# A start with x tiles 2 and 3 transposed by DMA, and K of both branches in pieces of 512, 512 and 256 columns, in a two-branch linear attention kernel

## The chip, the cores and the metric

The kernel runs on one core of a Trainium2 chip. The metric is the device time of one execution in microseconds (us). Each round of experiments ran on a chip of its own, beside its own runs of the kernel before. The profile also tells the granted clock, the share of full speed that TensorE was allowed. One execution of each kernel is also traced.

## The reference

Two attention branches A and B read the same x (2048 rows of 640, bf16) and differ in their weights. Each has 32 heads of 20 features. A gate per row mixes them.

```python
def branch(x, wqkv, wo):                      # A and B alike
    q, k, v = heads(x @ wqkv)
    phi = lambda t: jnp.where(t > 0, t + 1, jnp.exp(t)) + 1e-6
    pq, pk = phi(q), phi(k)
    kv  = jnp.einsum("bhsd,bhse->bhde", pk, v)
    z   = jnp.einsum("bhsd->bhd", pk)
    num = jnp.einsum("bhqd,bhde->bhqe", pq, kv)
    den = jnp.einsum("bhqd,bhd->bhq", pq, z)[..., None] + 1e-6
    return rows(num / den) @ wo
# x = A_x for both branches
g = sigmoid((x * gate_w).sum(-1, keepdims=True))
return g * branch(x, A_wqkv, A_wo) + (1 - g) * branch(x, B_wqkv, B_wo)
```

## The kernel before

x is cut into 16 tiles of 128 rows. The stages, in TensorE's order, are: K of every tile and branch (x^T times the K weights, then the feature map phi on ScalarE and VectorE); G = phi(K)^T x, summed over all tiles; M and WP, which fold the V weights and the output weights into G; the queries; the denominators (`dens`); the factors 1/den (`scale_q`); and the final products (`final`). A small list scheduler in the program orders the operations of each engine and picks PSUM banks. Each DMA has a semaphore of its own.

The start: single loads for tiles 0 to 3 of x, which TensorE transposes, and DMA transposes for the rest.

```python
        load_wk("SP", 4)
        load_x("ACT", 2)
        load_x("SP", 3)
        for c0, c1 in ((0, 1), (1, 3), (3, 5)):
            dma("SP", "wkB%d" % c0, WK["B"][:, c0:c1, :], weights("B", D, c0, c1), ...)
        for b in range(1, NB):            # x^T of tiles 4 to 15, four tiles each
            dma("SP", "xt%d" % b, XT[:, :, 512 * b : 512 * b + 512], ..., transpose=True)
        # ... constants, then the rows of x, four tiles each, then V, output and Q weights
```

K of a tile is made in two pieces of 320 columns for each branch (G of one k runs over all 16 tiles; its code is in the whole kernel below):

```python
        def k_part(X, t, tile, cs, chain=False):
            # ...
            def steps():
                return [
                    (PS[:, tile.banks[h], 0:HALF], XT[:, c, xc], WK[X][:, c, HALF * h : HALF * h + HALF], c == 0, c == NC - 1, None)
                    for h, c in order
                ]
```

The part that will matter although the change doesn't touch it: the factor 1/den is made by VectorE (`rc`), written to a DRAM scratch by SyncE (`fw`), read back spread over the partitions (`fr`), and multiplied into the query features by VectorE.

```python
            sch.op("DVE", rec, 1740, reads=[(ds,)], writes=[(ds,)], name="rc%d" % b)
            dma("SP", "fw%d" % b, rep..., lambda: RC[...], ...)            # factor <- RC
            dma("SP", "fr%d" % b, lambda: RX[...], rep..., ...)            # RX <- factor
            # for each piece and branch: VectorE, PQ = PQ * RX  ("ml")
# ... and the order of the second half of the kernel:
        d01 = dens(0)
        scale_q(0, d01, 2)
        queries(2)
        queries(3)
        scale_q(1, d01, 2)
        d23 = dens(2)
        finals(0)
```

In VectorE's program the multiplies of `scale_q(0)`, which wait for the read-back, stand in front of later feature maps of `queries(2)` and `queries(3)`, and those free TensorE's PSUM banks and feed `dens(2)`. The chain in experiment 1 shows them run in that order.

Of the kernel before, what the change touches and what calls it, by code (L numbers as in the profile page):

```python
# [19 lines left out]
D = 640  # L20
# [295 lines left out]
def bass_gated_mix__linear_attn_block__linear_attn_block__prompt_kernel(nc, A_x, A_wqkv, A_wo, B_x, B_wqkv, B_wo, gate_w, out):  # L316
# [6 lines left out]
    with ExitStack() as es:  # L323
        E = es.enter_context

        def sb(name, shape, dtype=dt.bfloat16):
            return E(nc.sbuf_tensor(name, shape, dtype))
# [4 lines left out]
        WK = {X: sb("WK" + X, [128, NC, D]) for X in XS}  # L332
        WV = {X: sb("WV" + X, [128, NC * D + 88]) for X in XS}
        WO = {X: sb("WO" + X, [128, 5, D]) for X in XS}
        FE = {X: sb("FE" + X, [128, NT * D]) for X in XS}
        PK = {X: FE[X][:, :].rearrange("p (t f) -> p t f", f=D) for X in XS}
        PQ = {X: FE[X][:, :].rearrange("p (k s) -> p k s", s=S) for X in XS}
# [102 lines left out]
        load_x("ACT", 2)  # L440
        load_x("SP", 3)
# [5 lines left out]
        for b in range(1, NB):  # L447
            dma(
                "SP", "xt%d" % b, XT[:, :, 512 * b : 512 * b + 512], xin[512 * b : 512 * b + 512, :],
                writes=[("XT", t) for t in range(4 * b, 4 * b + 4)], us=3.3, transpose=True,  # L450
            )
        dma("SP", "consts", CB[:, :], cap[:, :], writes=[("CB",)], us=0.3)
        dma("SP", "gw", GWB[:, :], gate_w.partition_broadcast(128), writes=[("GWB",)], us=0.4)
        for b in range(1, NB):
            dma(
                "SP", "xn_%d" % b, XN[:, 4 * b : 4 * b + 4, 0:D],
                xin[512 * b : 512 * b + 512, :].rearrange("(t p) f -> p t f", p=128),
                writes=[("XN", t) for t in range(4 * b, 4 * b + 4)], us=2.0,
            )
# [27 lines left out]
        def transpose_x(t):  # L487
# [11 lines left out]
            for c0, c1 in ((0, 2), (2, NC)) if t < 2 else ((0, NC),):  # L499
                sch.op(  # L500
                    "DVE",
                    lambda e, c0=c0, c1=c1: e.tensor_copy(  # L502
                        XT[:, c0:c1, 128 * t : 128 * t + 128],
                        PSB[:, tt.banks[0], 128 * c0 : 128 * c1].rearrange("p (c f) -> p c f", f=128),
                    ),
                    _dve_ns(128 * (c1 - c0)), reads=[(tt,)], writes=[("XTC", t, c) for c in range(c0, c1)], name="xev%d" % t,
                )
# [29 lines left out]
        def k_part(X, t, tile, cs, chain=False):  # L537
# [3 lines left out]
            def steps():  # L541
# [6 lines left out]
                "k%s%d_%d" % (X, t, cs[0]), steps, ([("XTC", t, c) for c in cs] if t < 4 else [("XT", t)]) + [("WK", X, c) for c in cs], [(tile,)], len(cs) * (D + 12),  # L548
                after=at[0] if chain else None,
            )  # L550
            if chain:
                at[0] = o

        gone = {}

        def g_unit(X, k):
            tile = _Tile(2)

            def steps():
                r = []  # L560
                for t in range(NT):
# [5 lines left out]
            gone[X] = mms(  # L567
                "g%s%d" % (X, k), steps,
                [("F", X, "k", t) for t in range(NT)] + [("XN", t) for t in range(NT)] + [("XN1",)], [(tile,)], NT * (D + 13),
            )  # L570
# [125 lines left out]
        def q_unit(X, b, k):  # L696
# [8 lines left out]
            over = [("F", X, "k", t) for t in range(span[0] // D, span[-1] // D + 1)]  # L705
# [7 lines left out]
            mms("q%s%d%d" % (X, b, k), steps, ([("XT", t) for t in range(4 * b, 4 * b + 4)] if b else [("XTC", t, c) for t in range(4) for c in range(NC)]) + [("WQ", X)], [(tile,)], NC * 518, after=gone[X])  # L713
# [151 lines left out]
        transpose_x(2)  # L865
# [3 lines left out]
        transpose_x(3)  # L869
        for t in (2, 3):  # L870
            first("A", *[(t, c) for c in range(NC)])
            phi_k("A", t, kt["A", t])
        for t in range(4):
            first("B", *[(t, c) for c in range(NC)])
            phi_k("B", t, kt["B", t])
        for b in range(1, NB):
            for X in XS:
                for t in range(4 * b, 4 * b + 4):
                    tile = _Tile(2)
                    k_part(X, t, tile, list(range(NC)), chain=True)  # L880
                    phi_k(X, t, tile)
# [85 lines left out]
```

## Time and profile before

| | before |
|---|---|
| time known at the prediction, three executions | 196.35, 194.47, 194.06 us, median 194.47 |
| execution that was traced | 193.3 us, span 191.5 us |
| TensorE busy | 187.0 us, 98% of the span |
| VectorE, ScalarE busy | 128.6 us (67%), 74.8 us (39%) |

Read the busy shares first: TensorE is at 98%, nothing else is near. Then read the chain that ended last. The prediction shows its beginning; here is its end (start us, duration us, what):

```profile
188.18 0.40 ACT TS L831
...
188.61 0.38 DVE OL L837
```

The last VectorE instruction ends at 188.61 + 0.38 = 188.99 us, and the span ends at 191.5. The 2.51 us between them are the last output's store and what comes after it. (The spans are printed to 0.1 us, so each such tail, as this stretch is called below, is good to 0.05 us.)

### The profile page before, as it was taken

The numbers are of one execution on the slowest core, as the hardware profiler recorded it, in microseconds if no ns is written. First come the engines' busy times: TensorE is split into PE (matmuls) and PEld (weight loads), VectorE is DVE, ScalarE is ACT, GpSimd is POOL, SyncE is SP. The second block draws the span as 40 slices with busy tenths as digits, with TensorE's granted clock in tenths as the row PEclk, the third lists the DMA queues.
The fourth block names the chain that finished last, engine by engine and source line by source line (L and its number), as shares of the span: only waits on it lengthen the run. The fifth ranks groups of instructions, "written<-read, shape, count | busy, mean of one in ns | idle before, by whom it ended". The sixth has DMA issues, their size and how long they took to land.

```text
span 191.5 us, 3302 instructions
## 1 busy us (share of the span) xinstructions
PE 187.0 (98%) x1370; PEld 131.8 (69%) x1370; DVE 128.6 (67%) x247; ACT 74.8 (39%) x115; POOL 8.2 (4%) x14
## 2 busy tenths in 40 slices
PE   7899999999999999999999999999999999999993
PEld 3677777777888888888855666455556677777773
DVE  1298888888700008996179997896999969923332
ACT  2154545555311111203255478565554331333232
POOL 8900000000000000000000000000000000000000
PEclk9999999999999999999999999999999999999999
DMA  5999999980011411121543004665000173221122
GB/s 173 330 211 185 180 388 364 311 216 17 3 34 34 38 34 34 34 38 34 38 90 107 0 24 172 162 223 170 0 0 0 38 218 104 78 96 64 39 72 68
DMA packets 30784, 21.17 MB, mean 111 GB/s; under 512 B 15538, under 2 KB 30514, under 8 KB 30770
## 3 DMA queue, kind: packets, MB, share of 16 engines
q1 hardware_dynamic: 30050, 20.23, 40.8%
q10 hardware_dynamic: 720, 0.74, 1.1%
q8 instruction: 11, 0.18, 0.4%
q14 instruction: 3, 0.02, 0.0%
HBM read 12.05 MB, written 5.31 MB: 91 GB/s over the span
## 4 chain that ended last, share of the span: by engine, by line
PE 95%; DMA 2%; ACTq 0%; DVE 0%; ACT 0%; issue 0%
PE ps L398 95%; DMA XN<-in_A_x_dram 2%; PE ps L493 1%; ACTq L387 0%; ACT TS L831 0%; DVE OL L837 0%; DVE XT L502 0%
## 5 line engine op out<-in xcount | busy, mean ns | idle before, releaser
L521 ACT ACTIVATE EK<-ps 128x640 bf16<-128x640 f32 x32 | 22.4, 703 | 24.1 <-PE ps L398 24.1
L715 ACT ACTIVATE EK<-ps 128x512 bf16<-128x512 f32 x40 | 23.9, 597 | 18.4 <-PE ps L398 17.0
L831 ACT ACTIVATE TS<-ps,GA 128x640 f32<-128x640 f32 (+2 forms) x18 | 13.2, 734 | 29.6 <-PE ps L398 29.6
L398 PE MATMUL ps<-WPB,FEB 128*128 128x320 bf16 (+1 forms) x165 | 24.7, 295 | 0.0
L398 PE MATMUL ps<-WPA,FEA 128*128 128x320 bf16 (+1 forms) x165 | 24.7, 295 | 0.0
L398 PE MATMUL ps<-WKA,XT 128*128 128x320 bf16 x160 | 22.9, 299 | 0.5 <-DMA WKA<-in_A_wqkv_dram 0.3
L398 PE MATMUL ps<-XT,WQA 128*128 128x512 bf16 x100 | 22.8, 380 | 0.0
L398 PE MATMUL ps<-XT,WQB 128*128 128x512 bf16 x100 | 22.7, 379 | 0.0
L398 PE MATMUL ps<-XN,FEB 128*128 128x320 bf16 (+1 forms) x160 | 22.5, 300 | 0.0
L398 PE MATMUL ps<-WKB,XT 128*128 128x320 bf16 x160 | 22.4, 299 | 0.0
L837 DVE SCALAR_TENSOR_TENSOR OS<-ps,GA,TS 128x640 bf16<-128x640 f32 x15 | 13.0, 867 | 13.4 <-PE ps L398 12.8
L398 PE MATMUL ps<-XN,FEA 128*128 128x320 bf16 (+1 forms) x160 | 22.0, 300 | 0.0
L572 ACT ACTIVATE GS<-ps 128x640 bf16<-128x640 f32 x10 | 7.0, 703 | 36.7 <-PE ps L398 36.7
L398 PEld LDWEIGHTS ps<-XN,FEA 128*128 128x128 bf16 x160 | 18.8, 117 | 3.0
L398 PEld LDWEIGHTS ps<-XN,FEB 128*128 128x128 bf16 x160 | 18.7, 118 | 3.0
L398 PEld LDWEIGHTS ps<-WKA,XT 128*128 128x128 bf16 x160 | 15.4, 98 | 7.0 <-DVE XT L502 1.3
L398 PEld LDWEIGHTS ps<-WPA,FEA 128*128 128x128 bf16 x165 | 15.9, 98 | 6.1
L398 PEld LDWEIGHTS ps<-WPB,FEB 128*128 128x128 bf16 x165 | 15.8, 98 | 6.2 <-ACT TS L831 0.4
L398 PEld LDWEIGHTS ps<-WKB,XT 128*128 128x128 bf16 x160 | 15.7, 98 | 6.1
L398 PEld LDWEIGHTS ps<-XT,WQA 128*128 128x128 bf16 x100 | 11.6, 118 | 9.4 <-issue 0.4
L398 PEld LDWEIGHTS ps<-XT,WQB 128*128 128x128 bf16 x100 | 11.7, 117 | 9.2
L677 DVE SCALAR_TENSOR_TENSOR GP<-XN,GWB 128x640 bf16<-128x640 bf16 x16 | 13.2, 828 | 4.1 <-PE ps L398 3.5
(56 smaller groups left out, 153.9 us busy)
## 6 DMA issues: line engine op xcount, KB each, us to landing
out_dram<-OS SPq DMA_DIRECT2D x15, 160.0 KB, 1.8
XN<-in_A_x_dram SPq DMA_DIRECT2D x3, 640.0 KB, 8.1
factor<-RC SPq DMA_DIRECT2D x4, 256.0 KB, 2.8
RX<-factor SPq DMA_DIRECT2D x4, 256.0 KB, 3.2
WVA<-in_A_wqkv_dram SPq DMA_DIRECT2D x1, 800.0 KB, 10.3
WQA<-in_A_wqkv_dram SPq DMA_DIRECT2D x1, 800.0 KB, 11.5
WVB<-in_B_wqkv_dram SPq DMA_DIRECT2D x1, 800.0 KB, 11.8
WQB<-in_B_wqkv_dram SPq DMA_DIRECT2D x1, 800.0 KB, 13.5
```

The source lines that it names most:

```text
L398: ins = pe.matmul(o, l, r, start=a, stop=z, tile_position=tp, skip_group_check=True)
L493: ins = pe.transpose(PSB[:, tt.banks[0], 128 * c : 128 * c + 128], XN[:, t, 128 * c : 128 * c + 128], IDN[:, :])
L521: "ACT", lambda e: e.activation(ek2(), pair(tile, HALF), ACT.Exp),
L572: "ACT", lambda e: e.activation(GS[:, k, :].rearrange("p (h f) -> p h f", f=HALF), pair(tile, HALF), ACT.Copy),
L677: lambda e, t=t: e.scalar_tensor_tensor(out=GP[:, :], in0=XN[:, t, 0:D], scalar=1.0, in1=GWB[:, :], op0=ALU.mult, op1=ALU.mult, accum_out= ...
L715: "ACT", lambda e: e.activation(ek(), PS[:, tile.banks[0], :], ACT.Exp), _act_ns(512), reads=[(tile,)],
L831: "ACT", lambda e, acc=acc, t_ap=t_ap: e.activation(t_ap(), acc(), ACT.Copy, scale=GA[:, 0, t : t + 1]),
L837: lambda e, acc=acc, t_ap=t_ap, o_ap=o_ap: e.scalar_tensor_tensor(out=o_ap(), in0=acc(), scalar=GA[:, 1, t : t + 1], in1=t_ap(), op0=ALU.m ...
```

## The change

The intent has two parts. At the start, x^T of tiles 2 and 3 comes by DMA transpose rather than from TensorE, with K of both branches of tiles 0 and 1 first to give that transpose time. From tile 4 on, K of both branches is made per tile in pieces of 512 (A), 512 (B) and 256 columns (the last 128 of each), which needs fewer matmuls. G is cut in two parts so that it can begin before the last tile's features are there. The core of the diff, with cuts marked:

```diff
+        WKJ = sb("WK", [128, 2, NC, D])
+        WK = {X: WKJ[:, x, :, :] for x, X in enumerate(XS)}
...
-        load_x("ACT", 2)
-        load_x("SP", 3)
...
-        for b in range(1, NB):
+        for t0, t1 in ((2, 4), (4, 8), (8, 12), (12, 16)):
             dma(
-                "SP", "xt%d" % b, XT[:, :, 512 * b : 512 * b + 512], ...
+                "SP", "xt%d" % t0, XT[:, :, 128 * t0 : 128 * t1], ...          # transpose; the rows of x alike
...
+        def k_both(t):
...
+            for part in ("A", "B", "AB"):
...
+                n = 512 if len(part) == 1 else 256
...
+                def wk(c, part=part, x=x):
+                    return WKJ[:, x, c, 0:512] if len(part) == 1 else WKJ[:, :, c, 512:D]
...
-                for t in range(NT):                                            # G
+                for t in range(lo, hi):
...
+            for lo, hi in ((0, NT - 4), (NT - 4, NT)):
...
-        transpose_x(2)
         for t in (0, 1):
             first("A", (t, 4))
             phi_k("A", t, kt["A", t])
-        transpose_x(3)
-        for t in (2, 3):
...
+        for X, ts in (("B", (0, 1)), ("A", (2, 3)), ("B", (2, 3))):
+            for t in ts:
+                first(X, *[(t, c) for c in range(NC)])
+                phi_k(X, t, kt[X, t])
+        for t in range(4, NT):
+            k_both(t)
```

More of the change, by code (lines that the diff above doesn't have):

```diff
@@ L331, in bass_gated_mix__linear_attn_block__linear_attn_block__prompt_kernel @@
         WQ = {X: sb("WQ" + X, [128, NC, D]) for X in XS}
-        WK = {X: sb("WK" + X, [128, NC, D]) for X in XS}
+        WKJ = sb("WK", [128, 2, NC, D])
+        WK = {X: WKJ[:, x, :, :] for x, X in enumerate(XS)}
         WV = {X: sb("WV" + X, [128, NC * D + 88]) for X in XS}
         WO = {X: sb("WO" + X, [128, 5, D]) for X in XS}
-        FE = {X: sb("FE" + X, [128, NT * D]) for X in XS}
-        PK = {X: FE[X][:, :].rearrange("p (t f) -> p t f", f=D) for X in XS}
-        PQ = {X: FE[X][:, :].rearrange("p (k s) -> p k s", s=S) for X in XS}
+        FE = sb("FE", [128, 2, NT * D])
+        PKJ = FE[:, :, :].rearrange("p x (t f) -> p x t f", f=D)
+        PK = {X: PKJ[:, x, :, :] for x, X in enumerate(XS)}
+        PQ = {X: FE[:, x, :].rearrange("p (k s) -> p k s", s=S) for x, X in enumerate(XS)}
         WP = {X: sb("WP" + X, [128, NC, D]) for X in XS}
@@ L446, in bass_gated_mix__linear_attn_block__linear_attn_block__prompt_kernel @@
             )
-        for b in range(1, NB):
+        for t0, t1 in ((2, 4), (4, 8), (8, 12), (12, 16)):
             dma(
-                "SP", "xt%d" % b, XT[:, :, 512 * b : 512 * b + 512], xin[512 * b : 512 * b + 512, :],
-                writes=[("XT", t) for t in range(4 * b, 4 * b + 4)], us=3.3, transpose=True,
+                "SP", "xt%d" % t0, XT[:, :, 128 * t0 : 128 * t1], xin[128 * t0 : 128 * t1, :],
+                writes=[("XT", t) for t in range(t0, t1)], us=0.82 * (t1 - t0), transpose=True,
             )
@@ L453, in bass_gated_mix__linear_attn_block__linear_attn_block__prompt_kernel @@
         dma("SP", "gw", GWB[:, :], gate_w.partition_broadcast(128), writes=[("GWB",)], us=0.4)
-        for b in range(1, NB):
+        for t0, t1 in ((2, 4), (4, 8), (8, 12), (12, 16)):
             dma(
-                "SP", "xn_%d" % b, XN[:, 4 * b : 4 * b + 4, 0:D],
-                xin[512 * b : 512 * b + 512, :].rearrange("(t p) f -> p t f", p=128),
-                writes=[("XN", t) for t in range(4 * b, 4 * b + 4)], us=2.0,
+                "SP", "xn_%d" % t0, XN[:, t0:t1, 0:D], xin[128 * t0 : 128 * t1, :].rearrange("(t p) f -> p t f", p=128),
+                writes=[("XN", t) for t in range(t0, t1)], us=0.5 * (t1 - t0),
             )
@@ L498, in transpose_x @@
             )
-            for c0, c1 in ((0, 2), (2, NC)) if t < 2 else ((0, NC),):
+            for c0, c1 in ((0, 2), (2, NC)):
                 sch.op(
@@ L547, in k_part @@
             o = mms(
-                "k%s%d_%d" % (X, t, cs[0]), steps, ([("XTC", t, c) for c in cs] if t < 4 else [("XT", t)]) + [("WK", X, c) for c in cs], [(tile,)], len(cs) * (D + 12),
+                "k%s%d_%d" % (X, t, cs[0]), steps, ([("XTC", t, c) for c in cs] if t < 2 else [("XT", t)]) + [("WK", X, c) for c in cs], [(tile,)], len(cs) * (D + 12),
                 after=at[0] if chain else None,
@@ L552, in k_part, with two, steps, ps @@
                 at[0] = o
+        def k_both(t):
+            xc = slice(128 * t, 128 * t + 128)
+            for part in ("A", "B", "AB"):
+                tile = _Tile(1)
+                es = _Tile(1, ring["ek"])
+                x = XS.index(part[0])
+                n = 512 if len(part) == 1 else 256
+                def two(v, part=part):
+                    return v if len(part) == 1 else v.rearrange("p (x f) -> p x f", x=2)
+                def wk(c, part=part, x=x):
+                    return WKJ[:, x, c, 0:512] if len(part) == 1 else WKJ[:, :, c, 512:D]
+                def steps(tile=tile, n=n, two=two, wk=wk):
+                    return [
+                        (two(PS[:, tile.banks[0], 0:n]), XT[:, c, xc], wk(c), c == 0, c == NC - 1, None)
+                        for c in range(NC)
+                    ]
+                at[0] = mms(
+                    "k%s%d" % (part, t), steps, [("XT", t)] + [("WK", X, c) for X in part for c in range(NC)], [(tile,)], NC * (n + 6), after=at[0],
+                )
+                def ps(tile=tile, n=n):
+                    return PS[:, tile.banks[0], 0:n]
+                def ek(es=es, n=n):
+                    return EK[:, es.slot, 0:n]
+                sch.op(
+                    "ACT", lambda e, ps=ps, ek=ek: e.activation(ek(), ps(), ACT.Exp), _act_ns(n), reads=[(tile,)], writes=[(es,)],
+                    name="ek%s%d" % (part, t),
+                )
+                sch.op(
+                    "DVE", lambda e, ek=ek: e.tensor_scalar(ek(), ek(), 1.0, EPS, op0=ALU.min, op1=ALU.add), _dve_ns(n, 4),
+                    reads=[(es,)], writes=[(es,)], name="tk%s%d" % (part, t),
+                )
+                def sk(e, ps=ps, ek=ek, part=part, x=x, two=two):
+                    out = PKJ[:, x, t, 0:512] if len(part) == 1 else PKJ[:, :, t, 512:D]
+                    return e.scalar_tensor_tensor(out=out, in0=two(ps()), scalar=0.0, in1=two(ek()), op0=ALU.max, op1=ALU.add)
+                sch.op(
+                    "DVE", sk, _dve_ns(n), reads=[(tile,), (es,)],
+                    writes=[("F", X, "k" if len(part) == 1 else "k5", t) for X in part], name="sk%s%d" % (part, t),
+                )
         gone = {}
@@ L557, in g_unit, with steps @@
             tile = _Tile(2)
-            def steps():
+            def steps(lo, hi):
                 r = []
-                for t in range(NT):
+                for t in range(lo, hi):
                     w = PK[X][:, t, k : D : NC]
@@ L565, in steps @@
                 return r
-            gone[X] = mms(
-                "g%s%d" % (X, k), steps,
-                [("F", X, "k", t) for t in range(NT)] + [("XN", t) for t in range(NT)] + [("XN1",)], [(tile,)], NT * (D + 13),
-            )
+            for lo, hi in ((0, NT - 4), (NT - 4, NT)):
+                gone[X] = mms(
+                    "g%s%d_%d" % (X, k, lo), lambda lo=lo, hi=hi: steps(lo, hi),
+                    [("F", X, w, t) for w in ("k", "k5") for t in range(lo, hi)] + [("XN", t) for t in range(lo, hi)] + [("XN1",)],
+                    [(tile,)], (hi - lo) * (D + 13),
+                )
             sch.op(
@@ L704, in q_unit @@
             span = range(S * k + 512 * b, S * k + 512 * b + 512)
-            over = [("F", X, "k", t) for t in range(span[0] // D, span[-1] // D + 1)]
+            over = [("F", X, w, t) for w in ("k", "k5") for t in range(span[0] // D, span[-1] // D + 1)]
             def steps():
@@ L711, in steps @@
                 ]
-            mms("q%s%d%d" % (X, b, k), steps, ([("XT", t) for t in range(4 * b, 4 * b + 4)] if b else [("XTC", t, c) for t in range(4) for c in range(NC)]) + [("WQ", X)], [(tile,)], NC * 518, after=gone[X])
+            mms("q%s%d%d" % (X, b, k), steps, [("XTC", t, c) for t in range(4 * b, 2) for c in range(NC)] + [("XT", t) for t in range(max(2, 4 * b), 4 * b + 4)] + [("WQ", X)], [(tile,)], NC * 518, after=gone[X])
             sch.op(
@@ L868, in bass_gated_mix__linear_attn_block__linear_attn_block__prompt_kernel @@
             phi_k("A", t, kt["A", t])
-        transpose_x(3)
-        for t in (2, 3):
-            first("A", *[(t, c) for c in range(NC)])
-            phi_k("A", t, kt["A", t])
-        for t in range(4):
-            first("B", *[(t, c) for c in range(NC)])
-            phi_k("B", t, kt["B", t])
-        for b in range(1, NB):
-            for X in XS:
-                for t in range(4 * b, 4 * b + 4):
-                    tile = _Tile(2)
-                    k_part(X, t, tile, list(range(NC)), chain=True)
-                    phi_k(X, t, tile)
+        for X, ts in (("B", (0, 1)), ("A", (2, 3)), ("B", (2, 3))):
[4 more added lines that the diff above has]
+            k_both(t)
         for k in range(NC):
```

## The prediction

> **What bounds the kernel now.** I read the busy shares first, then the chain of work that ended last in order of time, then the matmuls in order of time, then the queue of SyncE and its transfers' landings. Shares, from the page:
>
> ```profile
> PE 187.0 (98%) x1370; PEld 131.8 (69%) x1370; DVE 128.6 (67%) x247; ACT 74.8 (39%) x115; POOL 8.2 (4%) x14
> ```
>
> The chain of the kernel before (start us, duration us, what), its pieces from the landing of x's tile 1 on:
>
> ```profile
> 1.66 3.97 DMA XN<-in_A_x_dram
> 5.62 0.05 issue
> 5.67 0.47 PE ps L493 x5
> 6.14 0.02 issue
> 6.16 0.30 DVE XT L502
> 6.46 0.05 issue
> 6.51 1.80 PE ps L398 x12
> 8.31 0.28 PE ps L493 x5
> 8.59 0.54 PE ps L398 x4
> 9.14 0.28 PE ps L493 x5
> 9.41 178.75 PE ps L398 x1317
> ```
>
> Two things to see. From 6.51 us to 188.16 us TensorE never waits: this stretch changes only if its own instructions change, or if a new wait enters it. And the two pieces "L493 x5" at 8.31 and 9.14 are the TensorE transposes of x tiles 2 and 3: 0.28 us each, on the path. The start up to 6.51 us hangs on the landing of tile 1 of x (5.62 us).
>
> The same kernel's matmuls in order of time (start, modelled duration, shape, count), the lines that give the spacing of back-to-back matmuls:
>
> ```profile
> 17.40 5.60 PE L398 MATMUL ps<-WKA,XT 128*128 128x320 bf16 x40
> 22.84 5.60 PE L398 MATMUL ps<-WKB,XT 128*128 128x320 bf16 x40
> ...
> 96.15 5.56 PE L398 MATMUL ps<-XT,WQA 128*128 128x512 bf16 x25
> 101.55 5.56 PE L398 MATMUL ps<-XT,WQB 128*128 128x512 bf16 x25
> ...
> 186.95 0.51 PE L398 MATMUL ps<-WPA,FEA 128*128 128x160 bf16 x5
> 187.29 0.51 PE L398 MATMUL ps<-WPB,FEB 128*128 128x160 bf16 x5
> ```
>
> Subtract starts, not durations (the ends overlap): 5.44 us over 40 is 136 ns per 320 columns; 5.40 over 25 is 216 ns per 512; 0.34 over 5 is 68 ns per 160. At the granted clock of 1.00 (2.4 GHz in the program's constant) the columns alone are 133.3, 213.3 and 66.7 ns, so each matmul pays some 2.6 ns whatever its width. The 160-column line also says that a weight load (98 ns long in its row) doesn't set the spacing of narrower matmuls: it lies beside the matmul.
>
> VectorE's rows of the costliest groups, for the new 512- and 256-column pieces:
>
> ```profile
> L530 DVE SCALAR_TENSOR_TENSOR FEA<-ps,EK 128x640 bf16<-128x640 f32 x16 | 13.2, 824 | 0.5
> L724 DVE SCALAR_TENSOR_TENSOR FEA<-ps,EK 128x512 bf16<-128x512 f32 x20 | 13.4, 683 | 0.4
> L719 DVE TENSOR_SCALAR EK<-EK 128x512 bf16<-128x512 bf16 x40 | 10.8, 286 | 2.5 <-ACT EK L715 1.8
> L525 DVE TENSOR_SCALAR EK<-EK 128x640 bf16<-128x640 bf16 x32 | 10.4, 325 | 5.2 <-ACT EK L521 5.2
> ```
>
> **What the Trainium skill says.** "TensorE: Matmul & The Clock Gate", section "Wait — 56ns, not 53.3ns?", gives a warm spacing of N / 2.4 GHz plus a fixed 2.5 ns or so per matmul; the 2.6 ns above agrees. The same page, "Back-to-back issue gap", gives some 81 ns for 128 columns once weight loads are counted; the trace disagrees (68 ns at 160 columns; five 128-column transposes in 0.28 us, 56 ns each), and I use the trace. "Perfetto Trace Analysis", section "DMA Instruction — HWDGE (DVE, Sync)", says the window shown for a DMA is descriptor generation, not data movement. The trace agrees: the first x^T transpose is issued at 4.52 us, its 256-byte packets start near 8.7 us and it lands at 13.3 us. "DMA: Bandwidth & Descriptors", section "HWDGE ordering" under "Queues, rings and completion order", says that a queue's descriptors are taken in ring order on each engine, so what stands ahead in SyncE's queue delays what follows.
>
> **The change part by part.**
>
> 1. *Transposes of tiles 2, 3 go from TensorE to DMA.* Removed: two groups of five matmuls, 2 x 0.28 = 0.56 us, all on the path. Also removed: two VectorE copies of 0.49 us and two PSUM tiles, off the path, worth nothing.
>
> 2. *K of tiles 4 to 15 in 512, 512 and 256 columns.* Before, a tile of both branches is 20 x 135.85 (5.434 us over 40) = 2717 ns. After, 10 x 216 + 5 x (106.7 + 2.6) = 2160 + 546.5 = 2706.5 ns. The same 6,400 columns, five fixed costs fewer: 10.5 to 13 ns a tile, 12 tiles: 0.13 to 0.16 us. That is all that wider matmuls can bring, since the columns don't change.
>
> 3. *Order at the start.* K of A, tiles 0 and 1, then K of B, tiles 0 and 1 (20 x 135.85 = 2.72 us), then tiles 2 and 3. The built order has no other change on TensorE. Same matmuls, no gain by itself; it buys time for the DMA transpose, but asks for B's K weights earlier.
>
> 4. *G of each k in two parts*, tiles 0 to 11 and 12 to 15. No instruction changes; it lets G begin before the last tile's features are there. The first part is 24 x 136 = 3.27 us long, during which ScalarE and VectorE finish tile 15. The last part of tile 15 needs an exp (256 columns, some 0.38 us from the slope of 597 and 703 ns) and three or four VectorE instructions (some 2 us with the queue): it fits.
>
> 5. *Loads.* Two x loads (160 KB each) leave the front of the queues, so SyncE reaches B's weights one issue (0.43 us) earlier; the x rows come later in bulk, needed only at G (50 us).
>
> Sum: 0.56 + 0.15 = 0.71 us off a path with no other wait, less whatever new wait appears.
>
> **The rivals.**
>
> *A. TensorE waits for the new DMA transpose.* K of A tile 2 comes up at 6.51 + 12 x 0.136 + 4 x 0.136 + 20 x 0.136 = 11.4 us. Before, the first transpose (four tiles) landed at 13.3 us, which would be a stall of nearly 2 us; but it stood behind 320 KB more of loads. The DMA engines move some 350 GB/s from 3 to 9 us, so 328 kB is 0.94 us: B's last weights had landed at 10.0 us and should land near 9.1. The two-tile transpose is 1280 packets of 256 bytes, half of 2560. By the counts of small packets per half microsecond, the old transpose had moved 1280 about 1.8 us after its first packet at 8.7 us; the new one starts near 7.8 us and so has moved its data near 9.6 us. The old one landed 1.6 us after its last packet by that count, so the new one lands between 9.6 and 11.2 us. My estimate is that it makes it by 0.2 to 1.8 us; one chance in five of a stall, at most some 1 us, which would eat the gain.
>
> ```profile
> XT<-in_A_x_dram SPq DMA_TRANSPOSE x1, 8.8
> ```
>
> (issue to landing of that first transpose, asked for the moment of its issue.)
>
> *B. TensorE waits for B's K weights.* Before, the three loads landed at 8.3, 9.1 and 10.0 us (issue plus 5.2, 5.6 and 6.0 us). Moved up by 0.94 us: 7.3, 8.2, 9.1. Needed: first piece at 6.51 + 16 x 0.136 = 8.7 us, second 0.27 us later, third at 9.5 us. It fits, by 0.4 us at the least; a small stall of some 0.2 us is possible, and would be paid back from A, whose need moves with it.
>
> *C. VectorE becomes the bound of the K stage.* Per tile before: 2 x (825 + 325) = 2300 ns. After: 2 x (286 + 686) plus the 256-column pair, which by the slopes (1.09 and 0.30 ns a column) is 408 + 208: 2560 ns, against 2706 of TensorE. 95% busy by this sum, though in the trace neighbouring instructions overlap by some 0.06 us. If the three-part pieces were 10% dearer than this, VectorE would fall behind by some 0.1 us a tile, 1.3 us over 12 tiles: the eight PSUM banks (eight parts, 7.2 us of TensorE work, before a bank is used again in the planned order) and G's first part of 3.27 us swallow that. So a bound here would hardly show.
>
> *D. The 256-column matmuls with two strided 128-column runs are slower than by columns.* If each took the 118 ns of a longer weight load, 60 x 9 = 0.5 us. The 160-column spacing speaks against it.
>
> *E. Something larger, over 2% (3.9 us).* TensorE's columns are unchanged, so there is nothing to remove; a loss of this size would need a stall that none of A to D reaches.
>
> **Range and chances.** Before: 194.47 us. Minus 0.71, plus some 0.05 for the chance of A or B: 193.8 us. The three times of before spread from 194.06 to 196.35, so the median itself is good to some 0.4 us; with all of the gain and a low draw 193.1; with a stall of 1 us or a high draw 194.8. Both ends are far inside 2%.
>
> **What would show it.** In the changed profile: the chain has the five-matmul transposes twice instead of four times; K of tiles 4 to 15 takes 12 x 2.706 = 32.5 us where it took 32.6; G begins about 0.7 us earlier than 50.00 us, relative to the same landing of tile 1; and the list of waits shows no wait of TensorE on x^T or B's weights after 6.5 us. Wrong would be: a wait on the x^T transpose at about 11.4 us (A), on B's weights near 8.7 us (B), matmuls of 256 columns spaced by more than 110 ns (D), VectorE solid in the K stage with TensorE waiting for its banks (C), or tile 1 of x landing at a different time, which moves everything.

## The result, and the profile after

| | before | after |
|---|---|---|
| median of six executions | 194.09 us | 192.26 us |
| range | 193.58 to 196.35 | 191.98 to 192.35 |
| traced execution: time, span | 193.3, 191.5 | 192.26, 190.5 |
| TensorE instructions of matmul kind | 1370 | 1300 |

Ratios are the mean time of one kernel's fast runs over that of the other's of the same rounds, so they aren't quite the ratio of the medians. Executions over 1.5% slower than the fastest of the same kernel are left out of the means. Here the ratio is 0.9888, with a 95% interval of 0.9841 to 0.9935. So the change is 1.1% faster. The medians differ by 1.83 us, where 0.71 was predicted, and 192.26 lies below the predicted range. The outputs of all twelve experiments agree with the reference's.

The chain of the kernel after, its pieces from the landing of x's tile 1 on:

```profile
1.65 4.10 DMA XN<-in_A_x_dram
...
5.79 0.47 PE ps L492 x5
...
6.63 180.89 PE ps L400 x1265
...
187.54 0.40 ACT TS L881
...
187.97 0.38 DVE OL L887
```

TensorE's stretch without a wait is 6.63 to 187.52 us now, one piece. The two pieces of five transposes that stood at 8.31 and 9.14 are gone. The chain hangs on the same landing as before, which came 0.12 us later in this execution. Its last instruction ends at 187.97 + 0.38 = 188.35, and the span ends at 190.5: 2.15 us, where before had 2.51.

The matmuls of the kernel after in order of time (start, modelled duration, shape, count, idle before):

```profile
6.63 42.95 PE L400 MATMUL ps<-WK,XT 128*128 128x320 bf16 x256 [0.17 <-DVE XT L501]
49.41 4.79 PE L400 MATMUL ps<-XN,FE 128*128 128x320 bf16 x34
```

From the start of the unbroken run to the first matmul of G it is 49.41 - 6.63 = 42.78 us. Before it was 50.00 - 6.51 = 43.49, with both numbers in the prediction. The difference is 0.71 us, the predicted sum. (The row counts 256 matmuls in one group; the group's shape is that of its first one.)

The new transpose in the kernel after's DMA issues, with the us from issue to landing:

```profile
XT<-in_A_x_dram SPq DMA_TRANSPOSE x1, 6.2
```

And the new VectorE pieces in its groups (busy us, mean ns of one, idle before):

```profile
L595 DVE SCALAR_TENSOR_TENSOR FE<-ps,EK 128x256 bf16<-128x256 f32 x12 | 5.0, 415 | 0.0
```

The transpose of tiles 2 and 3 was issued at 4.05 us and landed 6.2 us later, at 10.25 us. TensorE needed it at about 11.5. This is the dearer of the two VectorE instructions of a 256-column piece: it took 415 ns, where 408 was estimated, and VectorE had no idle time ahead of it. (The other one took 227 ns, where 208 was estimated.)

So every step of the predicted sum is there. In the two traces the whole difference of 1.0 us in span is: G 0.59 us earlier (0.71 less 0.12 for the later start), 0.06 us less in the stage from the first to the second group of denominator matmuls, and 0.4 us less after the last VectorE instruction. The medians differ by 0.8 us more than that. The question is what the other 1.1 us are.

### The profile page after: what moved, and what is told of

Same layout as the page of the kernel before. It is cut to its first block, busy times and chain, and to the rows that moved or that the text cites.

```text
span 190.5 us, 3227 instructions
## 1 busy us (share of the span) xinstructions
PE 186.7 (98%) x1300; PEld 125.5 (66%) x1300; DVE 129.5 (68%) x269; ACT 76.3 (40%) x127; POOL 8.2 (4%) x14
## 4 chain that ended last, share of the span: by engine, by line
PE 95%; DMA 2%; ACTq 0%; DVE 0%; ACT 0%; issue 0%
PE ps L400 95%; DMA XN<-in_A_x_dram 2%; ACTq L389 0%; PE ps L492 0%; ACT TS L881 0%; DVE OL L887 0%; DVE XT L501 0%
## 5 line engine op out<-in xcount | busy, mean ns | idle before, releaser
L400 PE MATMUL ps<-WK,XT 128*128 128x512 bf16 (+2 forms) x260 | 44.2, 332 | 0.2 <-DVE XT L501 0.2
L400 PE MATMUL ps<-XN,FE 128*128 128x320 bf16 x320 | 44.3, 300 | 0.0
L400 PEld LDWEIGHTS ps<-XN,FE 128*128 128x128 bf16 x320 | 37.5, 117 | 6.0
L400 PEld LDWEIGHTS ps<-WK,XT 128*128 128x128 bf16 x260 | 25.4, 98 | 19.0 <-DVE XT L501 1.0
L774 DVE SCALAR_TENSOR_TENSOR FE<-ps,EK 128x512 bf16<-128x512 f32 x40 | 26.9, 690 | 0.7
L400 PE MATMUL ps<-WPB,FE 128*128 128x320 bf16 (+1 forms) x165 | 24.7, 295 | 0.0
L400 PE MATMUL ps<-WPA,FE 128*128 128x320 bf16 (+1 forms) x165 | 24.7, 295 | 0.0
L585 ACT ACTIVATE EK<-ps 128x512 bf16<-128x512 f32 (+1 forms) x36 | 18.3, 526 | 13.8 <-PE ps L400 13.8
L595 DVE SCALAR_TENSOR_TENSOR FE<-ps,EK 128x512 bf16<-128x512 f32 (+1 forms) x36 | 20.5, 597 | 0.4
L400 PEld LDWEIGHTS ps<-WPA,FE 128*128 128x128 bf16 x165 | 15.9, 98 | 6.1
## 6 DMA issues: line engine op xcount, KB each, us to landing
WVA<-in_A_wqkv_dram SPq DMA_DIRECT2D x1, 800.0 KB, 10.7
WVB<-in_B_wqkv_dram SPq DMA_DIRECT2D x1, 800.0 KB, 11.2
```

What stands on the lines that cost most here:

```text
L400: ins = pe.matmul(o, l, r, start=a, stop=z, tile_position=tp, skip_group_check=True)
L585: "ACT", lambda e, ps=ps, ek=ek: e.activation(ek(), ps(), ACT.Exp), _act_ns(n), reads=[(tile,)], writes=[(es,)],
L595: return e.scalar_tensor_tensor(out=out, in0=two(ps()), scalar=0.0, in1=two(ek()), op0=ALU.max, op1=ALU.add)
L774: lambda e: e.scalar_tensor_tensor(out=dst, in0=PS[:, tile.banks[0], :], scalar=0.0, in1=ek(), op0=ALU.max, op1=ALU.add),
```

## The experiments

The expectations were written before each run and use their own numbering of the theories. In the first round the leading theory was that the loads of x tiles 2 and 3 sometimes land late in the kernel before, so that most of its executions lose time at the start that the traced one didn't lose. Its rivals were something after G, and chance.

The kernel before had 11 runs beside the first four kernels (median 194.01 us), 12 beside the second four (194.27, or 194.19 without the slow one) and 11 beside the third four (193.83).

### 1. The kernel before again

No edit.

> The kernel before once more, nothing edited. It asks how far its executions differ among themselves. Theory 1 (landing): before's TensorE transposes of x tiles 2 and 3 come up 0.25 and 1.3 us after those loads landed in the one traced execution (7.9 against 8.15 us, 7.7 against 8.97); in other executions the loads land later and TensorE waits some 0.3 to 1 us there. Then this kernel's times spread over 1 us or so, its mean lies some 0.5 us above the 193.3 of the traced execution, and a second trace may show a wait on x at about 8.2 us. Rival (chip or first-run noise): the 196.35 and the 194.47 were the first chip's runs; then on one chip the times agree within 0.3 us and lie near 193.3. Ratio to before 1.000 within 0.003 in both.

Measured: median 194.10 us (193.30 to 194.37), ratio 0.9982 [0.9942, 1.0022]. The traced execution took 194.29 us, with a span of 192.4, so this one is an ordinary, slower execution of the same program. Its chain, cut to where it leaves TensorE:

```profile
124.43 1.75 DVE RC L765
...
126.21 3.20 DMA factor<-RC
...
129.43 4.93 DMA RX<-factor
...
147.87 0.69 DVE FEB L724
...
148.61 40.45 PE ps L398 x315
```

This is a chain that the first trace didn't have. From 124.4 to 148.6 us the end hangs on the first factor: the reciprocal, the write, the read-back of 4.93 us, the multiplies, and then VectorE behind with the queries' feature maps. The matmuls of the same execution in order of time show what TensorE lost by it:

```profile
138.48 5.59 PE L398 MATMUL ps<-XT,WQB 128*128 128x512 bf16 x25 [0.45 <-DVE FEB L724]
...
145.56 1.52 PE L398 MATMUL ps<-WPB,FEB 128*128 128x320 bf16 x10
...
148.61 0.39 PE L398 MATMUL ps<-FEA,ZBDA 128*32 128x512 bf16 x2 [0.17 <-DVE FEB L724]
```

By the spacing of the matmuls ahead of them, these three begin 0.61, 0.30 and 0.24 us late. The view puts the first and the last down to VectorE: one wait for a PSUM bank, and one before the second denominators. A measure that takes in all such losses is the time from the start of the first denominators to the start of the second: 26.00 us here. It is 24.88 in the first trace of before and 24.82 in both traces of after. So this execution lost 1.18 us in the middle. On tile 2 of x there was a wait too, but a small one: the first of its transposes starts at 7.92 us, 0.11 us later than the spacing would have it, and the weight load ahead of it waited for that load. So the leading theory has 0.11 us to show in this trace, a tenth of the loss in the middle.

### 2. The kernel after again

No edit.

> The changed kernel once more, nothing edited, beside the kernel before on the same chip. Theory 1: ratio 0.991 to 0.993 (1.3 to 1.7 us, of which 0.7 us are removed transposes and fixed matmul costs and the rest a start that no longer depends on late x tiles), with a spread of its own times of 0.4 us at most. Rival (noise of the first chip): 0.7 to 1.0 us, ratio 0.995 to 0.9965.

Measured: median 192.19 us (191.89 to 192.25), ratio 0.9886 [0.9849, 0.9924]. The gain is real, and more than either theory forecast; the spread is small again.

The pair of these two traces closes the account. Spans 192.4 and 190.1 differ by 2.3 us. G begins at 49.78 and 49.05 (0.73 us), denominators to denominators takes 26.00 and 24.82 (1.18), and from the end of the last VectorE instruction to the end of the span it is 2.51 and 2.11 (0.40). The sum is 2.31 us.

### 3. The start part alone

After, with K of tiles 4 to 15 as before (joint tensors and G in two parts kept):

```diff
-        for t in range(4, NT):
-            k_both(t)
+        for b in range(1, NB):
+            for X in XS:
+                for t in range(4 * b, 4 * b + 4):
+                    tile = _Tile(2)
+                    k_part(X, t, tile, list(range(NC)), chain=True)
+                    phi_k(X, t, tile)
```

> Only the start of the change: tiles 2 and 3 by DMA transpose and B's K of tiles 0 and 1 first; tiles 4 to 15 keep ten 320-column matmuls a branch. Theory 1: keeps the 0.56 us of transposes and all of the unexplained 0.5 to 0.9 us: 1.2 to 1.5 us below before, narrow spread. Rival (the excess comes from the K stage or from G's split): 0.5 to 0.6 us below before, with the wide spread of before.

Measured: six times that fall in two groups: 192.29, 192.19 and 192.54 us, and 195.38, 194.30 and 194.76. Ratio 0.9953 [0.989, 1.0015]. The loads of tiles 2 and 3 are gone from the front here, yet the spread is as wide as that of before. So those loads aren't needed for a wide spread, and as the main cause the leading theory was given up. The two spreads need not have one cause, though: 195.38 (slow) and 194.76 have a mean granted clock of 0.991, the other four 0.999 to 1.00, and so have all of before's 11 runs of this round (0.998 to 1.00). None of the three long executions was traced. The traced execution (192.29, one of the fast group) had a tail of 2.11 us after VectorE's end, like the kernel after.

### 4. The K part alone

After, with the old start (the inverse of the start's diff; the loads of tiles 2 and 3 are in front again):

```diff
+        load_x("ACT", 2)
+        load_x("SP", 3)
...
+        transpose_x(2)
...
+        transpose_x(3)
```

> Only the K stage of the change: 512, 512 and 256 columns from tile 4 on and G in two parts; the start is the old one with four TensorE transposes. Theory 1: 0.15 us below before, with before's wide spread. Rival (the excess comes from the K stage): 0.7 to 1.1 us below before and a narrow spread.

Measured: median 193.36 us; five executions between 193.19 and 193.42, one at 194.30; ratio 0.9955 [0.9915, 0.9995]. The old start with its loads, and a narrow spread. The gain is 0.65 us by the medians, where 0.15 was predicted for this part. The tail is 2.56 us, that of before. Denominators to denominators takes 24.82 us.

### What the first four showed, and a second theory

The traces hold DMA packets that fetch instructions. On queue q8, which moves 16 KB in a packet, there are 11 in before and 10 in after. The instruction queues in the page of before (packets, MB, share of the engines' time):

```profile
q8 instruction: 11, 0.18, 0.4%
q14 instruction: 3, 0.02, 0.0%
```

And in the page of the kernel after:

```profile
q8 instruction: 10, 0.16, 0.3%
q14 instruction: 5, 0.04, 0.1%
```

The Trainium skill, "Runtime: NRT & Kernel Launch", section "Instruction fetch mechanics", says that an engine's instructions are refilled in blocks of 16 KiB, which is 256 instructions, over a DMA queue of the sequencer, and that this is mostly hidden. The trace agrees with the size on q8 (on q14 the packets are of 8 KB), and q8 fits TensorE: 2 x 1370 matmuls and weight loads are 10.7 blocks, 2 x 1300 are 10.2. That q8 is TensorE's is inferred from this, and from where its packets go when only TensorE's instructions change (below).

In a stretch of the DMA view cut to the first read-back of each traced execution, the packet is there in both traces of before and not in after. Before, 129.85 to 133.55 us:

```profile
q8 instruction: 1, 0.02, 1.6%
```

The second trace of before, 129.4 to 134.4 us:

```profile
q8 instruction: 1, 0.02, 1.1%
```

In the kernel after, 129.0 to 131.75 us, the same view has the read-back's own queue alone:

```profile
q1 hardware_dynamic: 1050, 0.52, 65.7%
```

Hence the second theory. A 16 KB instruction packet that falls into the read-back of the first factor lengthens it, VectorE falls behind, and TensorE pays in some executions. The change moves that packet: 70 matmuls fewer, each with a weight load, are 140 instructions, over half a block. At 216 ns a query matmul, 70 of them are 15 us, so the packet at 130 should move to some 145 (an estimate from the spacing), and it is at 144. The rival was that the stall in the middle is chance, or that the K stage or the PSUM banks cause it. The second four kernels tell these apart by changing only the number of K matmuls, some 100 us ahead of the read-back. A third point was the tail: the kernels with the short one have one DMA more on SyncE.

### 5. Before, with 60 matmuls more

K of tiles 4 to 6 in halves of 160 columns. The same columns, more instructions: it should be slower by 60 x 2.6 ns = 0.16 us if only TensorE's time counts.

```diff
+                    for lo, hi in (((0, 160), (160, HALF)) if t in (4, 5, 6) else ((0, HALF),))
```

> The kernel before with K of tiles 4 to 6 in 160-column halves: 60 matmuls more, the same columns, 0.16 us dearer. In the traces so far one 16 KB instruction fetch on a DMA ring falls at 130 to 132 us in the two traces of before and in that of the start alone, into the read-back of the first factor (2.7 to 4.9 us long there), and at 119 to 123 and 144 us in the K stage alone and in the changed kernel, outside it. Theory F (fetch): 60 matmuls more move the fetch to some 122 and 143 us; the first read-back lands in 2.7 to 2.8 us; times 193.3 to 193.6 with a spread of 0.3 us, 0.5 to 0.8 us under before although it does more. Rival B (something else of the K stage, PSUM banks or VectorE's pieces): still before's spread of 1 to 3 us and 0.16 us slower than before, 194.2.

Measured: median 193.75 us (five between 193.56 and 193.79, one 194.32), against 194.27 of before (194.19 without its slow run). Ratio 0.9981 [0.996, 1.0002]: equal times are just inside the interval, the 0.16 us of slowdown (a ratio of 1.0008) is not. More work on the engine that bounds the kernel, and the median is lower, with a narrower spread than before's 193.64 to 194.61. It is also 0.15 us above the range that the second theory (F) forecast. The packet now falls at 124 and 146 us, the read-back takes 3.0 us, and denominators to denominators takes 24.82.

### 6. The same, with one SyncE DMA more

The last bulk load of x rows is also cut in two.

```diff
-        for b in range(1, NB):
+        for t0, t1 in ((4, 8), (8, 12), (12, 14), (14, 16)):
```

> The same, with the last bulk load of x rows split in two, so that SyncE has one DMA more, as in the changed kernel. The end after the last VectorE instruction is 2.5 us long in the traces of before and of the K stage alone, 2.1 us in those of the changed kernel and of the start alone; SyncE's program has one instruction more in the latter. Theory S (length of SyncE's program): end of 2.1 us, 0.3 to 0.4 us under the kernel without the split. Rival (the end belongs to something else of the start, or to chance): the same time within 0.1 us and an end of 2.5 us.

Measured: median 193.67 us (192.93 to 195.56), ratio 0.9982 [0.9943, 1.0021]: on time alone inconclusive. (The packet is away from the read-back here too, and yet the times spread widely; 195.56 is one of the executions with a mean clock of 0.991.) The trace is clear on the tail: 2.15 us after VectorE's last instruction, where experiment 5 has 2.52. The start of this traced execution was late (TensorE's unbroken run began at 7.38 us, not 6.5), which hides the gain in its time.

### 7. The start part alone, with 70 matmuls more

Experiment 3, with halves of 160 columns in K of tiles 4 to 6 of both branches and tile 7 of A.

> Only the start of the change, with 70 K matmuls more by halving columns (0.18 us dearer), which by theory F moves the fetch to 122 and 143 us as in the changed kernel. Theory F: 192.3 to 192.5 us, spread 0.4 us; the first read-back 2.7 us. Rival B: as the start alone, 192.2 to 195.4, median 193.4 plus 0.2.

Measured: median 192.57 us (192.24 to 192.97), ratio 0.9918 [0.9897, 0.994]. The group at 194.3 to 195.4 that experiment 3 had is gone. The packet was at 132.5 us in experiment 3, half a microsecond after the landing of the read-back at 131.98; it is at 124 and 145 here. That the long executions of experiment 3 had it inside the read-back is not shown, and two of them had the lower clock; so this experiment is in line with the theory and no more.

### 8. The kernel after, with 70 matmuls more

The 512-column pieces of tiles 4 to 10 in two halves, so that TensorE's program is as long as that of before.

```diff
+                cut = len(part) == 1 and t < 11
...
+                    if cut:
+                        return [
+                            (PS[:, tile.banks[0], lo : lo + 256], XT[:, c, xc], wk(c)[:, lo : lo + 256], c == 0, c == NC - 1, None)
+                            for c in range(NC)
+                            for lo in (0, 256)
+                        ]
```

> The changed kernel with the 512-column K parts of tiles 4 to 10 as two of 256: 70 matmuls more, 0.18 us dearer; TensorE's program up to the query stage is then as long as before's to within one instruction, so by theory F the fetch falls at 129 to 131 us again, into the read-back. Theory F: the read-back is 3.5 to 5 us, times spread by 1 us or more, median 192.8 to 193.5. Rival B (K stage's own banks and pieces protect it): 192.4 us with a spread of 0.4.

Measured: median 192.79 us (192.53 to 193.25), ratio 0.9936 [0.9913, 0.9959], so 0.5% worse than the kernel after against its own runs of before, where the added matmuls are 70 x 2.6 ns = 0.18 us, or 0.1%. By the medians against each round's fast runs of before it is less: 1.40 us of gain where the kernel after had 1.82, so 0.42 us worse, 0.24 of them beyond the added matmuls. The two ratios' intervals overlap, so the size is loose; the traced stage is 0.21 us longer. The packet is back at 130 us, the read-back takes 4.0 us, and the chain runs through it again, as in the second trace of before:

```profile
129.09 4.00 DMA RX<-factor
...
147.33 40.45 PE ps L400 x315
```

The first multiply of VectorE by the factor, with its idle time in brackets, shows this in one line for each kernel: before,

```profile
133.49 0.83 DVE L783 TENSOR_TENSOR FEA<-FEA,RX 128x1280 bf16<-128x1280 bf16 x1 [1.54 <-DMA RX<-factor]
```

the second trace of before,

```profile
134.38 0.83 DVE L783 TENSOR_TENSOR FEA<-FEA,RX 128x1280 bf16<-128x1280 bf16 x1 [2.66 <-DMA RX<-factor]
```

the kernel after,

```profile
131.77 3.03 DVE L833 TENSOR_TENSOR FE<-FE,RX 128x1280 bf16<-128x1280 bf16 x4 [0.41 <-DMA RX<-factor]
```

and the kernel after with the packet brought back:

```profile
133.11 3.03 DVE L841 TENSOR_TENSOR FE<-FE,RX 128x1280 bf16<-128x1280 bf16 x4 [1.70 <-DMA RX<-factor]
```

The eight kernels of the two rounds and the first pair together, one traced execution each. The packet's time is good to 1 us; the tail is from the end of VectorE's last instruction to the end of the span.

| kernel | q8 packets near, us | read-back: issue, us to landing | VectorE idle for it | denominators to denominators | tail |
|---|---|---|---|---|---|
| before, first trace | 130 | 129.90, 3.6 | 1.54 | 24.88 | 2.51 |
| before again | 131 | 129.43, 4.9 | 2.66 | 26.00 | 2.51 |
| after + 70 matmuls | 130 | 129.09, 4.0 | 1.70 | 25.03 | 2.08 |
| start part alone | 132 | 129.28, 2.7 | 0.58 | 24.82 | 2.11 |
| after, first trace | 123, 144 | 129.03, 2.7 | 0.41 | 24.82 | 2.15 |
| after again | 122, 144 | 128.59, 2.7 | 0.28 | 24.82 | 2.11 |
| K part alone | 119, 144 | 129.59, 2.8 | 0.33 | 24.82 | 2.56 |
| before + 60 matmuls | 124, 146 | 130.46, 3.0 | 1.04 | 24.82 | 2.52 |
| the same, SyncE + 1 DMA | 124, 146 | 130.80, 2.8 | 0.69 | 24.82 | 2.15 |
| start part + 70 matmuls | 124, 145 | 129.79, 2.8 | 0.52 | 24.82 | 2.13 |

Where the packet falls inside the read-back, and only there, the read-back takes 3.6 to 4.9 us rather than 2.7 to 3.0, and the stage is longer than 24.82 us. The same start, the same K pieces, and before as well as after occur on both sides of this line, so the number of TensorE's instructions ahead decides it. How one 16 KB packet holds up hundreds of small ones is not shown in full, but the second trace of before has a hint. From 133.25 to 134.4 us the last packets trickle, some ten in a quarter of a microsecond, and the packets keep 7.6% of the 16 DMA engines busy, which is 1.2 engines. It looks as if one engine were left to finish its share alone. The trace doesn't name the engine of a packet, so this stays an inference.

### 9 to 12. The other parts of the change

These four ask what the G split and the loads at the front are worth, and whether x tile 1, on which the start hangs, can come earlier.

**9. G in one part.**

```diff
-            for lo, hi in ((0, NT - 4), (NT - 4, NT)):
+            for lo, hi in ((0, NT),):
```

> The changed kernel with G of each k in one part, as before. The step of the prediction on test: G's first part hides the features of tile 15. In the changed trace the last feature instruction of tile 15 ends at 51.2 us, while TensorE is at G from 49.4 us on. My theory: G now waits until 51.2 us, 1.8 us, time 193.9 to 194.1. Rival (the split was needless, G's operands are there in time): 192.2.

Measured: median 194.19 us, ratio 1.0021 [1.0006, 1.0037]. The whole gain is gone. The matmuls in order of time show the wait for tile 15's features:

```profile
51.06 9.19 PE L400 MATMUL ps<-XN,FE 128*128 128x320 bf16 x66 [1.67 <-DVE FE L595]
```

So the split carries no gain by itself, but without it TensorE stands for 1.67 us until VectorE has finished the features of tile 15.

**10. x tile 1 ahead of A's first K weights, on ScalarE's queue.**

```diff
+        load_x("ACT", 1)
         load_wk("ACT", 0)
         load_wk("SP", 1)
-        load_x("ACT", 1)
```

> The changed kernel with the load of x tile 1 ahead of A's K weights 0 on ScalarE's queue. The chain of the changed kernel begins with that load: issued at 1.65 us, landed at 5.75. Theory: issued at 1.17 it lands near 5.0; A's first weights land near 4.8 instead of 4.3; TensorE's unbroken run begins near 6.2 us instead of 6.3 to 6.6; 191.8 to 192.1 us. Rival: the weights then hold up TensorE by as much, 192.2.

Measured: median 194.72 us, ratio 1.0053 [1.0032, 1.0074]: slower. TensorE waits 1.6 us for the K weights that were pushed back. After that its 320-column matmuls stand up to 267 ns apart until 9.2 us, where 136 ns is usual: from its unbroken start to G it takes 51.42 - 8.22 = 43.20 us, 0.42 more than the kernel after.

**11. x tile 1 second on SyncE, A's second K weights on ScalarE.**

```diff
         load_wk("ACT", 0)
-        load_wk("SP", 1)
-        load_x("ACT", 1)
+        load_x("SP", 1)
+        load_wk("ACT", 1)
```

> The changed kernel with x tile 1 as the second load of SyncE's queue and A's K weights 1 third on ScalarE's instead. Theory: x tile 1 lands near 4.6, weights 1 near 5.4 us; TensorE's unbroken run begins near 6.1 us; 191.7 to 192.0. Rival: weights 1 hold up TensorE, 192.2 or more.

Measured: median 192.97 us, with two of six at 194.7; ratio 0.9979 [0.9941, 1.0017]. The waits of the traced execution are 0.6 us on A's K weights, and others on B's, whose last load landed at 10.33 us. From the unbroken start to G it takes 50.17 - 6.74 = 43.43 us, so the waits on B's weights cost 0.65 us there. This is rival B of the prediction, brought about by one load's place.

**12. The kernel after, with the loads of x tiles 2 and 3 in front again**, although nothing at the start needs them.

```diff
+        load_x("ACT", 2)
+        load_x("SP", 3)
...
-        for t0, t1 in ((2, 4), (4, 8), (8, 12), (12, 16)):
+        for t0, t1 in ((4, 8), (8, 12), (12, 16)):
```

> The changed kernel with the row loads of x tiles 2 and 3 at the front of the queues again, where the kernel before has them (their bulk load is left out); TensorE does not need them there. On test: steps 5, A and B of the prediction, that 320 KB less ahead is what lets B's weights and the transpose land in time. Theory: everything behind lands some 0.9 us later: the transpose of tiles 2 and 3 near 11.2 us, needed at 11.5; B's last weights near 10 us, needed at 9.6; a wait of TensorE on B's weights of 0.2 to 0.5 us, 192.4 to 192.8 us. Rival: nothing waits, 192.2.

Measured: median 193.16 us (192.48 to 194.83), ratio 0.9973 [0.9939, 1.0008]. In the traced execution (194.65 us) x tile 1 landed 5.07 us after its issue and TensorE stood 1.75 us for it, where it waited 0.16 and 0.31 in the two traces of after:

```profile
6.76 0.70 PE L494 MATMUL ps<-IDN,XN 128*128 128x128 bf16 x5 [1.75 <-DMA XN<-in_A_x_dram]
```

The wait on B's weights that was expected isn't there. The stretch after the wait was slower too: 51.79 - 7.85 = 43.94 us from its unbroken start to G, where the kernel after takes 42.78. The page says why: the granted clock, in tenths for 40 slices of the span, is down in the second slice.

```profile
PEclk9799999999999999999999999999999999999999
```

Asked microsecond by microsecond, the clock is 0.50 from 6.8 to 10.2 us, and 1.00 before and after. Half speed from 7.85 to 10.2 us costs some 1.2 us (an estimate), close to the 1.16 us of difference. What lowered it is not shown; it fell just as TensorE resumed after the wait. One stretch of 3.4 us at half speed makes a mean clock of 0.991 over the span. That is the very mean of ten executions, of the kernels of experiments 3, 6, 10, 11 and 12 and once of before. So a start of this kind is the likely reason for these long times, which no instruction fetch has to explain; only one of them was traced.

So the two loads in front may cost time at the start in some executions. The K part alone and experiment 5 have the same two loads and were narrow in five of six, and of before's 34 runs beside the experiments only one has the lower clock. How much of before's spread is theirs stays open.

None of these kernels beats the kernel after.

## Why the prediction was wrong, point by point

**Step 1, two groups of transposes: right.** The chain lost both. (The prediction's "twice instead of four times" counts the program's groups; in the chain of before three stand, and in that of after one.) The start part alone has 49.46 - 6.47 = 42.99 us from its unbroken start to G, 0.50 less than before, with 0.56 predicted. (One matmul of this run starts 0.05 us late, at 7.61 us, which makes up the difference.)

**Step 2, K in 512, 512 and 256 columns: right.** Tile 4 begins at 6.63 + 76 x 0.1358 = 16.95 us (the 76 matmuls of 320 columns left of tiles 0 to 3, at the measured spacing). From there to G the kernel after takes (49.41 - 16.95) / 12 = 2.705 us a tile, with 2.7065 predicted.

**Steps 3 to 5 and rivals A to D: right.** B's weights landed at 7.1, 8.05 and 9.0 us (7.3, 8.2 and 9.1 estimated), x^T at 10.25 (9.6 to 11.2 estimated). In the K stage VectorE never made TensorE wait. Step 4's estimate that the split gives time for the last features fits too, and experiment 9 shows that it was needed.

**The step that failed is the sum: "0.56 + 0.15 = 0.71 us off a path with no other wait", with rival E's "there is nothing to remove".** The 0.71 us were there to the hundredth. But the path of before has another wait in most executions, and more time behind its last instruction, and the change takes both away. Two terms were missing:

1. *The stall behind the first factor's read-back.* The stage is 0.06 us longer in one trace of before and 1.18 in the other. On average the stall is the difference of before and experiment 5, plus the 0.16 us of its added matmuls: by the medians of fast runs 0.44 + 0.16 = 0.60 us, by the ratio 0.37 + 0.16 = 0.53 us, with an interval that reaches from about 0.1 to 0.9. That it goes and comes with the instruction packet is shown in both directions, by experiment 5 (moved away) and experiment 8 (moved back).
2. *The tail.* From VectorE's end to the end of the span it is 2.51 to 2.56 us in the four traces of programs with before's number of DMAs on SyncE, and 2.08 to 2.17 in all ten with one more, some 0.4 us less. Experiments 5 and 6 differ in this alone. In nine of the ten a q14 instruction packet falls 1.8 to 2.0 us after VectorE's end; in those with the long tail, and in experiment 3, none is seen between there and the very end of the span. That a fetch of SyncE's last instructions makes the tail is therefore only a guess; what the runs show is that one DMA more on SyncE shortens it.

Together: 0.71 + 0.4 + 0.5 to 0.6 is 1.6 to 1.7 us. The medians of the first round of experiments differ by 194.01 - 192.19 = 1.82. What is left is inside the uncertainty of the second term; waits on x tile 2 at the start, of which one trace of before shows 0.11 us, may be part of it. The ratio, being of means, gives 1.14%, or 2.2 us: before has single executions at 195.08 and 196.21 us (at a mean clock of 1.00), of which no trace exists, so what they lost is open.

**What could have been seen.** The trace of before was a lucky execution: 193.3 us, below all three of the times that the prediction started from. The prediction took its wait-free path from that execution and its base from the median, and these are not the same thing. From the traced execution the sum would have been 193.3 - 0.71 - 0.4 = 192.2, and the kernel after's twelve timed executions lie between 191.89 and 192.35. Had the base been 193.3, only the tail would have been missing. That trace also had VectorE idle 1.54 us for a read-back of 3.6 us, off the path there, and the stage was 0.06 us longer.

**The range and chances.** That both ends lie far inside 2% held. The one chance in five of a stall on the new transpose didn't come up, which two traces can't test. The range didn't hold, because it allowed for stalls that the change could add and not for those that before already had.

## What to carry to other kernels

Compare the time of the traced execution with the median before taking a base from one and a path from the other; if they differ by more than the gain in question, the trace may lack a wait that most executions have. Compare the mean clock of the executions as well, before giving their times one cause. A change in the number of instructions can move the time by its instruction fetches alone, so it should help to keep some slack around small transfers that the chain waits for (not tested here). When a part of a change gains more than its own instructions can give, pad the instruction count back to tell the part from its side effect.

## What the Trainium skill lacked or had wrong

- "Runtime: NRT & Kernel Launch", section "Instruction fetch mechanics", treats the fetch as mostly hidden. No wait of TensorE in these traces could be put down to its own fetch, so for the engine itself nothing here contradicts it. What the page lacks, and no other page found has, is what a fetch can cost a transfer of the kernel. With a 16 KB packet inside it, a 256 KB read-back took 3.6 to 4.9 us, and 2.7 to 3.0 without, and the kernel lost up to 1.18 us.
- No page found has the tail: one SyncE DMA more in the program, and the span ended 2.1 us after the last compute instruction, where it was 2.5.
- "TensorE: Matmul & The Clock Gate", section "Back-to-back issue gap": 81 ns for 128 columns in a stream of weight loads and matmuls. Here five transposes of 128 columns took 0.28 us (56 ns each), and 160 columns took 68 ns. The 512-column spacing was 216 ns, where that section has 131. What the same section gives as the gap of an isolated matmul, 56 and 216 ns, is what this stream shows.
